# A transformer block on one core: norm groups of 2, 4, 4, 2, 1 and a new issue order

## The chip, the cores and the metric

One core of a Trainium2 chip. The kernel is written in Tile (Python that emits the instructions of each engine). The metric is the device time of one execution in microseconds; the median of the runs shown counts. Engines: PE (matmuls) with its weight loads (PEld), DVE (VectorE), ACT (ScalarE), POOL (GpSimd), SP (SyncE, which here only issues DMAs).

## The reference

Sequence 2048, width 512, 32 heads of 16, MLP width 1792 over the sequence axis, bfloat16.

```python
mod = (silu(c) @ w_mod).reshape(1, 6, 1, 512)            # sa, ca, ga, sb, cb, gb
h = layernorm(x) * (1 + ca) + sa
q, k, v = split_heads(h @ wqkv)
# each position attends to 8 positions of its past, 2 apart (0, 2, ..., 14 back), masked at the start
x = x + ga * (softmax(q . k[pos - off] * 16**-0.5) @ v[pos - off]) @ wo
h = layernorm(layernorm(x) * (1 + cb) + sb)
u = gelu(einsum('bsd,sf->bdf', h, w1) + b1)              # mixes along the sequence
x = x + gb * (einsum('bdf,fs->bds', u, w2) + b2).transpose
```

## The kernel before

The 16 tiles of 128 positions are worked in five chunks of 2, 4, 4, 4 and 2 tiles (`SIZES`). A chunk goes through the stages whose names are used below; the digits are chunk and part, or tile:

- ln1s, ln1v (statistics), rstd1, nb1, n1 (the first layer norm), then the transposition of the normed tiles: tr and hT by PE in chunks 0 and 1, xt by a transposing DMA on SP in chunks 2 to 4;
- qkv (12 groups of matmuls a chunk, in chunk 0 two parts each) and ev (its eviction from PSUM, on ACT or DVE); halo copies the last 16 positions of k and v to the next chunk;
- qk: the product of q with 8 shifted copies of k, one wide TENSOR_TENSOR on DVE per quarter of the width; red adds it up over the head on PE in psL; max, sub, exp, esum, rcp, smB form the softmax; a2 (a DMA on SP or ACT) spreads the weights over partitions, vd (a DMA on SP) lays out v;
- pv: the product of the weights with v on DVE, pvacc its sum on PE, oev its eviction, wo the output projection on PE, with one matmul more by the identity that adds the residual, x1 its eviction with the row sum (a DVE variant adds the residual itself, and then wo leaves that matmul out: flag n);
- ln2q (sum of squares), ln2m (variance), rstd2, nb2, n2, aff (scale and shift by the modulation), ln3s, ln3v, rstd3, nb3, h3: the two further layer norms. ln2m, rstd, nb and aff work on a group of `GRP[ch]` tiles at once; tiles 14 and 15 (`LN2D`) take their statistics with bn_stats instead of ln2q and ln2m.

The MLP's first product is summed over the sequence in sweeps (mlp1_sweep_column_tile), as h3 tiles become ready; park stores a partial sum, padd adds it again, gelu follows. mlp2 forms the 16 output tiles, fin adds bias, gate and residual, st_out stores.

The modulation: modcols on PE give shift and scale of the first norm as columns (a1col scales the weights: wsc; sab goes through qvb to the biases of q and v), modrow0 and modrow1 give the other rows, which go through DRAM (st_row, ld_row) to all partitions. modrow1 reads three of the six blocks of w_mod, loaded to a region of gT that the MLP later uses.

The order of all this is written out by hand in `ORDER`, one token per operation. Each engine issues its own operations in that order and waits in order; SP does so with its DMAs. A suffix a, d, p or s takes the variant on ACT, DVE, POOL or SP; q splits a matmul into four of 32 columns; n leaves out a matmul; fill:n is n matmuls of 128 columns without use. PSUM has six buffers of one bank (ps), SBUF four for the wide products (big) and five for vd, and a pool's buffer is taken in the order of ORDER. `schedule` (lines 86 to 125) turns ORDER into the program; lines 397 to 410 are rstd and nb, 459 to 461 the loads of w_mod's rows, 497 to 507 the halo, 560 to 594 the rows, 851 to 889 x1 to aff. Nearly every instruction is recorded under line 142, the wrapper that issues it, so the profile is read by tile names and by order.

## Time and profile before

| | us |
|---|---|
| median of 3 runs | 206.71 |
| lowest, highest | 206.41, 206.78 |
| profiled execution, its own time | 207.27 |
| its span in the profile | 205.6 |
| PE, DVE, ACT, POOL busy | 192.8, 160.4, 127.4, 21.1 |
| mean granted TensorE clock | 0.992 |

The span runs from the first to the last recorded instruction; the 1.7 us between it and the execution's time lie around it. Times in the views count from the start of the span. A busy PE is not a PE at its peak: a matmul of 512 columns is recorded with 379 ns, but one starts every 216 ns. An instruction's wait is shown in square brackets with the one that released it.

### The profile page before, as it was taken

Reading aid. Unit: us, or ns where it says so; the run is one execution under the profiler, and the core shown is the slowest. Engines: PE = TensorE matmul, PEld = TensorE weight load, DVE = VectorE, ACT = ScalarE, POOL = GpSimd, SP = SyncE. Lnnn points to the kernel's source line nnn. Section 1 sums busy time; section 2 is a strip of 40 time slices with the busy share of each in tenths; the row PEclk is TensorE's granted clock in tenths of the full one; section 3 lists DMA queues with packets and bytes.
Section 4 is the critical chain, followed back from the end, with each engine's and each line's share of the span. In section 5 each row is a group of like instructions: output and inputs, shape, how many; then the busy total and the mean of one; then the engine's idle time right before and its main releaser. Section 6 shows DMA issues by size and latency. Waiting matters only on the chain.

```text
span 205.6 us, 4632 instructions
## 1 busy us (share of the span) xinstructions
PE 192.8 (94%) x1852; PEld 99.5 (48%) x1852; DVE 160.4 (78%) x251; ACT 127.4 (62%) x305; POOL 21.1 (10%) x46
## 2 busy tenths in 40 slices
...
PEclk9969999999999999999999999999999999999999
...
GB/s 153 334 377 351 67 226 143 231 223 224 187 113 263 342 207 247 212 45 153 53 154 300 20 76 279 190 130 356 282 336 223 26 26 26 77 25 29 146 96 51
DMA packets 54945, 35.95 MB, mean 175 GB/s; under 512 B 24460, under 2 KB 52236, under 8 KB 54924
## 3 DMA queue, kind: packets, MB, share of 16 engines
...
q10 hardware_dynamic: 1368, 0.23, 0.8%
q8 instruction: 14, 0.23, 0.5%
...
## 4 chain that ended last, share of the span: by engine, by line
PE 49%; ACT 19%; DVE 14%; DMA 7%; issue 6%; POOL 2%; SPq 1%; ACTq 0%; DVEq 0%; POOLq 0%
PE psS L142 48%; DVE big L142 8%; ACT junk L142 4%; ACT h L142 3%; DMA hT<-h 3%; DVE h L142 3%; ACT v_sb L142 2%; DMA xx<-in_A_x_dram 2%; ACT xx L142 2%; ACT o_sb L142 2%; POOL h L142 2%; DMA a2sb<-lsb 1%; ACT q_sb L142 1%; ACT gT L142 1%; ACT k_f L142 1%
## 5 line engine op out<-in xcount | busy, mean ns | idle before, releaser
L142 PEld LDWEIGHTS <-wst 128*128 128x128 bf16 (+1 forms) x446 | 35.3, 102 | 34.5 <-issue 3.0
L142 PE MATMUL psS<-h,wst 128*128 128x512 bf16 (+1 forms) x296 | 50.3, 379 | 0.0
L142 DVE TENSOR_TENSOR big<-a2sb,vD 128x4096 bf16<-128x4096 bf16 (+1 forms) x20 | 36.7, 1860 | 2.2 <-PE psL L142 1.9
L142 DVE TENSOR_TENSOR big<-q_sb,k_f 128x4096 bf16<-128x4096 bf16 (+1 forms) x20 | 36.6, 1864 | 0.0
L142 PE MATMUL psS<-hT,w_qkv 128*32 128x512 bf16 (+3 forms) x432 | 29.7, 346 | 0.9 <-DMA hT<-h 0.9
L142 DVE SCALAR_TENSOR_TENSOR h<-psS,bcol,rows_bc 128x512 f32<-128x512 f32 (+2 forms) x18 | 12.4, 691 | 21.6 <-PE psS L142 21.4
L142 PEld LDWEIGHTS <-w_qkv 128*32 128x32 bf16 (+1 forms) x474 | 19.6, 108 | 17.5 <-issue 5.7
L142 PE MATMUL psS<-gT,big 128*128 128x512 bf16 x112 | 24.8, 379 | 0.0
L142 PEld LDWEIGHTS <-big 128*128 128x128 bf16 x144 | 12.0, 97 | 15.0 <-DMA big<-in_w_mod_dram 0.9
L142 PE MATMUL psS<-woq,o_sb 128*32 128x512 bf16 (+1 forms) x136 | 16.7, 380 | 1.0 <-ACT o_sb L142 1.0
L142 ACT ACTIVATE gT<-psS,bcol 128x512 bf16<-128x512 f32 x14 | 8.9, 687 | 8.4 <-DVE psS L142 8.4
L142 ACT ACTIVATE junk<-xx 128x512 bf16<-128x512 bf16 x20 | 12.6, 629 | 2.3 <-DMA xx<-in_A_x_dram 1.6
L142 ACT ACTIVATE h<-xx,nb,rs 128x512 bf16<-128x512 bf16 x16 | 13.0, 815 | 1.5 <-DVE nb L142 1.4
L142 DVE TENSOR_TENSOR h<-h,xx 128x512 bf16<-128x512 f32 (+2 forms) x18 | 11.4, 633 | 3.2 <-DMA out_dram<-h 2.6
L142 DVE BATCH_NORM_STATS2 st<-xx 128x6 f32<-128x512 bf16 x15 | 9.8, 681 | 5.1 <-DMA xx<-in_A_x_dram 5.1
L142 DVE TENSOR_TENSOR psS<-psS,gT 128x512 f32<-128x512 f32 x14 | 9.5, 697 | 4.8 <-PE psS L142 4.8
L142 PE MATMUL psS<-hT,wst 128*128 128x256 bf16 (+1 forms) x64 | 12.8, 361 | 0.0
L142 PEld LDWEIGHTS <-group 128*32 128x32 bf16 x288 | 7.2, 96 | 11.6 <-issue 4.5
L142 DVE TENSOR_TENSOR h<-h,rows_bc 128x512 bf16<-128x512 bf16 (+2 forms) x20 | 11.5, 582 | 1.3 <-POOL h L142 0.4
L142 POOL TENSOR_SCALAR h<-xx,rs,nb 128x512 bf16<-128x512 bf16 x7 | 7.4, 1061 | 49.0 <-DVE nb L142 49.0
L142 ACT ACTIVATE v_sb<-psS,qvb 128x512 bf16<-128x512 f32 (+1 forms) x20 | 11.1, 595 | 1.4 <-PE psS L142 1.3
L142 PE MATMUL psS<-big,group 128*32 128x512 bf16 (+1 forms) x160 | 9.8, 339 | 2.0 <-DVE big L142 1.9
...
## 6 DMA issues: line engine op xcount, KB each, us to landing
...
```

Of the source, the lines that this page charges most:

```text
L142: r = fn(*a, **k)
```

## The change

ORDER is replaced as a whole, and with it which engine takes which operation: 62 operations change engine. GRP goes from (2, 2, 4, 1, 1) to (2, 4, 4, 2, 1). ln2q gets a variant on DVE. ln2m works with sums scaled by D, so that a single tile needs one instruction; rstd2 then scales by -1/D^2. The rows of w_mod for modrow1 are loaded by four DMAs of 128 rows of 3 KB (one per 128 inputs) instead of three of 512 rows of 1 KB. The halo copies get one more key of order. wo10 and wo11 leave out the residual matmul. The fillers are 41 + 18 at the start (35 + 14 before), 4 and 10 in between (3 and 15), 26 at the end (7). In ORDER below, the stretches at the start, around the affine step of chunk 1, around the last products, and the end are kept.

```diff
ORDER = """
-ident ld_x_1_4 act_table ln1s4:d ld_x1 ld_x0 ld_x_1_2 ln1s1:d ln1v1 ln1v4 ld_wmod1 ld_c cps ln1s0:d ln1s5:a ln1v5
-fill:35 ln1v0 fill:14 ln1s2:d silu_exp consts rstd1_0 nb1_0 n1_0:a ln1s3:d n1_1:p ln1v2 ln1v3 silu_dve rstd1_1 nb1_1
-n1_5:d n1_4:d modcols1 tr0_0 a1col ld_x_2_8 n1_3:d n1_2:a tr1_0 hT0_1:a ln1s9:d ld_wqkv1 tr1_2 hT0_0:a hT1_0:d hT0_2:a
-ld_x_2_6 ln1s6:d hT0_3:a qkv0_12 hT1_3:a wsc1_1:p ld_wqkv0 hT1_2:a ld_x_3_12 ln1s7:d hT1_1:a ln1s8:d ln1v8 ev0_12:a
-ld_wmod0 wsc1_2:p wsc1_3:p ln1v7 ln1v6 qkv0_10 ld_x_3_10 ln1s13:d ln1v13 qkv1_13 wsc0_3:a ln1v9 ev0_10:a qkv0_02
-qkv1_01 wsc0_0:p modcols0 rstd1_2 wsc0_1:p ln1s12:d ln1v12 wsc0_2:a nb1_2 sab:a qvb0 qvb_cp0:a ev1_01:a qkv0_00
-ln1s10:d ln1s11:d qkv1_11 ld_wqkv2 qvb1 wsc1_0:p ev0_00:a ln1v10 wsc2_2:a ev1_11:a qvb_cp1:a ev0_02:d ln1v11 halo0
-rstd1_3 qk0_2 qk0_0 qkv1_03 ev1_03:a qk0_1 ld_wmod2 qk0_3 qkv0_22 ev0_22:a nb1_3 modrow0 mrows0:a ld_wmod4 qkv0_20:q
-n1_6:a red0_0 n1_10:a red0_1 ld_wmod3 red0_2 red0_3 mask ev0_20:a qk1_1 ev1_13:a qkv1_00 ev1_00:a qkv1_02 qkv1_10
-n1_12:a max0 n1_7:p sub0 exp0 ld_wmod5 modrow1 ev1_02:a xt6 ld_wo2 esum0 qk1_3 ld_x_4_14 vd0_0 vd0_3 n1_9:p rcp0 smB0
-qkv1_12 mrows1 n1_8:p ev1_10:a qk1_0 qkv1_20 qkv1_23 xt8 vd0_2 a2_0_2:s qkv1_21:q qkv1_22:q ev1_12:a qk1_2 n1_11:a
-a2_0_1:a red1_0 qkv2_10:q qkv2_00:q red1_1 a2_0_3:s a2_0_0:s pv0_2 ln1s15:a ev1_22:a ev1_23:a st_row0 red1_2 red1_3
-ln1v15 wsc2_1:a ev1_20:a qkv2_12 ev2_10:a qkv2_02:q halo_v1:p qkv2_11 pv0_0 vd0_1 ev2_00:a ev1_21:a max1 pvacc0_2 sub1
-pv0_3 ld_wo3 pv0_1 ld_w1_0_896 ev2_12:a pvacc0_3 pvacc0_0 pvacc0_1 ln1s14:a qkv2_03:q qk2_0 st_row1 wsc2_0:a exp1
-ev2_02:a ev2_11:a ld_wo0 ln1v14 ld_row0 wsc2_3:p ld_wo1 esum1 woq_s rcp1 qkv2_01 rstd1_4 qkv2_22:q ev2_01:a xt10
...
-oev2_3:a x1_4:a ln2q4 max3 sub3:q exp3 pv2_2 ld_w2_4 pv2_0 qkv4_10 rstd3_0 halo_v4:p pvacc2_2 esum3 oev2_2:a pv2_1
-qkv4_20:q ln2m4 rcp3 qkv4_00:q n2_2:a vd3_1 vd3_2 ev4_20:a ev4_10:a aff2 smB3 nb3_0 qkv4_22:q h3_0:p ev4_00:a pvacc2_0
-oev2_0:a rstd2_4 nb2_4 pvacc2_1 oev2_1:a wo7 wo9 ln3s3:d ln3v3 vd3_0 n2_5:d fill:15 n2_4:d ev4_22:a ln3s2:a ln3v2
-a2_3_3:a aff4 rstd3_2 nb3_2 x1_9:a wo6 ln3s5:d h3_1:a ln3s4:d wo8 ln3v5 h3_3:p h3_2:a mlp1_0_0_0 mlp1_0_6_0 ln2q9
-vd3_3 x1_6:a ln3v4 mlp1_0_2_0 a2_3_2:s mlp1_0_1_0 a2_3_0:s a2_3_1:s pv3_3 x1_7:a rstd3_4 pvacc3_3 ln2q6 nb3_4 h3_4:a
...
-ld_w1_0_1408 ln3s7:d mlp1_0_7_0:q ln3v9 ln3v7 mlp1_0_8_0:q ld_w2_3 ln3v8 ln3s6:a ln3v6 wo13:qn red4_0 x1_12:a rstd3_6
-red4_1 red4_2 red4_3 max4 mlp1_0_10_0 ln2q10 ln2m11 nb3_6 h3_7:p x1_13:d sub4 exp4 esum4 mlp1_0_9_0 ln2m10 h3_9:a
-h3_8:d ln2q12 rcp4 smB4 mlp1_0_11_0 h3_6:p mlp1_0_11_4 mlp1_0_11_8 vd4_0 vd4_3 rstd2_11 nb2_11 n2_11:d mlp1_0_8_4
-ln2m12 rstd2_10 vd4_1 mlp1_0_7_4 mlp1_0_7_8 a2_4_3:a nb2_10 a2_4_1:a n2_10:d aff10 rstd2_12 mlp1_0_8_8 mlp1_0_10_4
-mlp1_0_9_4 ln2q13 park0_7:a park0_8:a aff11 mlp1_0_12_0 ln2m13 rstd2_13 a2_4_2:s a2_4_0:s pv4_2 nb2_13 pv4_1 nb2_12
-pv4_0 pv4_3 ln3s11:a mlp1_0_9_8 mlp1_0_10_8 ln3s10:d n2_13:a mlp1_0_12_4 ln3v11 n2_12:a ln3v10 park0_9:a park0_10:a
-ld_w1_0_1664 aff13 aff12 mlp1_0_12_8 pvacc4_0 pvacc4_1 oev4_0:a ld_w1_1_0 pvacc4_2 pvacc4_3 oev4_2:a park0_11:a
-mlp1_0_13_0 wo15 x1_15 ln2s15 wo14 rstd3_10 nb3_10 rstd3_11 ln2v15 ln3s12:a ln3v12 mlp1_0_13_4 mlp1_0_13_8 h3_10:p
-x1_14 inj1_6:n park0_12:a rstd2_15 park0_13:a ln3s13:d nb2_15 ln2s14 ln3v13 rstd3_12 nb3_12 n2_15:a inj1_5:qn inj1_0:n
-mlp1_1_0_6 mlp1_1_0_10 ln2v14 rstd2_14 ld_w1_1_640 inj1_1:n mlp1_1_5_6 aff15 ln3s15:a nb2_14 park1_0:+ n2_14:p aff14
...
-fin8_0 st_out8_0 fin11_0 st_out11_0 st_out14_0 fin13_0 st_out13_0 fin12_0 mlp2_15_0 fin15_0 st_out12_0 st_out15_0
-mlp2_15_2 mlp2_15_1 fin15_2 fill:7 fin15_1 st_out15_2 st_out15_1
...
+ident consts act_table ld_x_1_4 ln1s5:d ld_c ln1v5 ln1s4:d ln1v4 cps ld_x1 ln1s1:a fill:41 ld_x_1_2 ln1v1 silu_exp
+silu_dve ln1s2:a ld_x0 ln1s0:d ln1s3:d halo0 ln1v0 rstd1_0 fill:18 ln1v3 ld_wmod1 ln1v2 rstd1_1 nb1_0 n1_1:a n1_0:d
+nb1_1 n1_2:d n1_3:d ld_x_2_6 ld_wqkv1 ld_x_2_8 modcols1 n1_4:a a1col tr0_0 hT0_1:a hT0_3:a hT0_0:a ld_wqkv0 n1_5:d
+ln1s6:d tr1_0 ln1s7:d hT0_2:a wsc1_0:p hT1_0:a wsc1_2:p tr1_2 ld_wmod0 ln1s9:d wsc1_3:p ln1s8:d ln1v9 ln1v8 ln1v7
+ln1v6 qkv0_12 ld_x_3_10 hT1_1:a qkv0_10 ev0_12:d hT1_2:a rstd1_2 nb1_2 hT1_3:a qkv0_02 wsc0_0:p ld_wqkv2 ln1s10:d
+modcols0 ln1s11:d ln1v10 n1_7:a sab:a ld_x_4_14 n1_6:a qkv0_00 qvb0 n1_9:a qvb_cp0:d ln1v11 qkv1_10 ld_x_3_12 ev0_02:d
+ev0_00:a ld_wo1 ld_b1 ld_wrow2 ev1_10:a qkv1_00 qkv1_13 qk0_2 qvb1 n1_8:a qk0_3 qkv0_22:q qkv0_20:q ev0_10:a ld_wo2
+qk0_0 ld_wo0 red0_0 ld_wo3 ev1_00:a qkv1_03:q ln1s13:a ev1_13:a qk0_1 qk1_0 ld_wmod2 ld_wrow0 qvb_cp1:a ev0_22:a
+qkv1_02:q wsc0_2:p red0_1 red0_2 ln1v13 ev1_03:a ev0_20:a ld_wrow1 ev1_02:a red0_3 mask max0 wsc0_1:p qk1_3 wsc1_1:p
+ln1s12:a xt6 ld_wrow3 qkv1_11:q ev1_11:a qkv1_01 vd0_2 ev1_01:a qk1_1 vd0_1 qkv1_12 ev1_12:a sub0:q exp0 wsc2_3:a
+qkv1_22:q vd0_3 modrow0 esum0:q rcp0 smB0 ln1s15:a xt8 a2_0_2:s red1_0 ln1s14:a qkv1_21 qk1_2 a2_0_3:s qkv1_20 ln1v12
+a2_0_0:s mrows0:a a2_0_1:s rstd1_3 st_row0 modrow1 mrows1 vd0_0 red1_1 nb1_3 red1_2 red1_3 ln1v14 qkv2_13 n1_10:a
+ln1v15 rstd1_4 ld_row0 n1_13:a max1 nb1_4 wsc0_3:p pv0_3 qkv2_00:q qkv1_23 ev2_13:a ev1_20:a ev2_00:a sub1 exp1
+ev1_22:a qkv2_10 qkv2_03:q st_row1 ev2_10:a pv0_1 ev2_03:a ld_b2 wsc2_1:a pv0_2 n1_12:p pvacc0_2 pvacc0_3 esum1
+ev1_23:a pv0_0 qkv2_12 qk2_0 rcp1 pvacc0_0 n1_11:p ev1_21:a pvacc0_1 smB1 qkv2_01:q woq_s qk2_3 xt10 xt12 qkv2_11:q
+oev0_2:a qkv2_02:q oev0_0:a wo0 a2_1_3:s halo_v1:p vd1_1 ev2_01:a ev2_12:a a2_1_1:s ev2_11:a qk2_1 wo1:q wsc2_2:a
...
+biascols_cp:a rcp3 qkv4_10:q ev4_12:a n2_2:a pv2_0 pvacc2_0 oev2_2:a pvacc2_3 ln3v0 vd3_3 smB3 a2_3_3:s a2_3_1:a
+qkv4_22 pv2_1 a2_3_0:s qkv4_00:q n2_4:a oev2_3:a rstd3_0 fill:10 oev2_0:a pvacc2_1 ev4_22:a oev2_1:a wo9:q a2_3_2:s
+wo6:q ev4_00:a aff2 ln3s4:a wo8:q pv3_1 pvacc3_1 ln3s5:d nb3_0 ln3s2:d ln3v4 ln3s3:a x1_8:a ln3v3 ln3v5 wo7 ln3v2
+rstd3_2 ev4_10:d x1_6:a nb3_2 h3_3:d h3_2:d pv3_2 h3_1:p h3_0:p h3_4:a mlp1_0_0_0 mlp1_0_2_0 vd3_0 vd4_3 ln2q6:a
+ld_w2_3 pv3_0 x1_9:a qk4_0 mlp1_0_6_0 oev3_1:a mlp1_0_1_0 ln2q8:a h3_5:a x1_7:a mlp1_0_0_4 ln2q7:a ln2q9:a vd4_0
+park0_0:a ln2m6 rstd2_6 mlp1_0_1_4 park0_1:a mlp1_0_2_4 mlp1_0_3_0 mlp1_0_3_4 park0_2:a ld_w1_0_896 red4_0 pvacc3_2
...
+ln3v8 ln3v7 ln3v6 vd4_2 mlp1_0_9_0:q ln3v9 ln2q12:a x1_10:d rstd3_6 nb3_6 h3_6:a ln2q10:a x1_13:d ln2q13:a esum4 rcp4
+x1_11:d h3_9:a ln2m12 rstd2_12 smB4 a2_4_0:a mlp1_0_8_0 ld_w1_0_1408 mlp1_0_10_0 ln2q11:d ln2m10 nb2_12 n2_13:d
+a2_4_3:a n2_12:d mlp1_0_7_0 h3_7:p mlp1_0_9_4 mlp1_0_7_4 mlp1_0_12_0 mlp1_0_8_4 a2_4_2:s aff12 rstd2_10 h3_8:p
+mlp1_0_8_8 mlp1_0_7_8 nb2_10 n2_10:a park0_7:a mlp1_0_12_4 a2_4_1:s pv4_3 mlp1_0_10_4 mlp1_0_10_8 n2_11:a pv4_0
+mlp1_0_9_8 mlp1_0_11_0 mlp1_0_11_4 pv4_2 pv4_1 aff10 ln3s11:d mlp1_0_11_8 park0_8:a park0_9:a park0_10:a park0_11:a
+pvacc4_0 pvacc4_2 pvacc4_3 oev4_2:a mlp1_0_12_8:q ln3s10:d ln3v10 ln3v11 pvacc4_1 oev4_0:a inj1_1:n ld_w1_0_1664
+mlp1_0_13_0 wo14 x1_14 ln3s12:a rstd3_10 mlp1_0_13_4 nb3_10 h3_10:p ln3v12 wo15 ld_w1_1_0 ln3s13:a ln2s14 ln2v14
+ld_w1_1_640 x1_15 rstd2_14 nb2_14 n2_14:p ld_w2_1 mlp1_0_13_8 inj1_3:n ln2s15 park0_12:a ln2v15 park0_13:a inj1_6:n
...
+fin8_0 st_out8_0 fin10_0 st_out10_0 mlp2_13_0 fin12_0 st_out12_0 st_out9_0 fin13_0 st_out7_0 mlp2_11_0 fin11_0
+st_out13_0 mlp2_14_0 fin14_0 mlp2_15_0 st_out11_0 mlp2_15_2 fin15_0 st_out14_0 fin15_2 st_out15_0 mlp2_15_1 fill:26
+st_out15_2 fin15_1 st_out15_1
...
"""
@@ -276,7 +276,7 @@
     ESD=(4,),
     RAW=(0, 1),
     LN2D=(14, 15),
-    GRP=(2, 2, 4, 1, 1),
+    GRP=(2,4,4,2,1),
     XDMA=(2, 3, 4),
     XG=2,
     INJ=(1,),
@@ -394,13 +394,13 @@
                                                op0=ALU.mult, op1=ALU.subtract, reverse1=True)
         add("dve", 0.15, fv, reads=[("stt", l, st)], writes=[("mv", l, st)], name=name[:3] + "v" + name[4:])
 
-    def ln_rstd(l, g0, n, name, var=None, vreads=None):
+    def ln_rstd(l, g0, n, name, vreads=None, vscale=1.0):
         mv, lv, rs, nb = (ln_t[k, l] for k in ("mv", "lv", "rs", "nb"))
         sl = slice(g0, g0 + n)
-        var = mv[:, sl, 1] if var is None else var
+        var = mv[:, sl, 1]
 
         def fa():
-            nc.scalar.activation(lv[:, sl, 0], var, ACT.Ln, bias=epscol[:, 0:1])
+            nc.scalar.activation(lv[:, sl, 0], var, ACT.Ln, scale=vscale, bias=epscol[:, 0:1])
             nc.scalar.activation(rs[:, sl, 0], lv[:, sl, 0], ACT.Exp, scale=-0.5)
         reads = [("mv", l, st) for st in range(g0, g0 + n)] if vreads is None else vreads
         add("act", 0.54, fa, reads=reads + ["ident", "act_table"], writes=[("rs", l, g0)], name="rstd" + name)
@@ -456,9 +456,8 @@
     dma(rowB, wmod_view[:, :, 2 * D:3 * D], D * D * 2, [], [("wst", 1)], "ld_wmod2")
     for l in range(4):
         dma(woq[32 * l:32 * l + 32, :, :], wo_view[l], 32 * 4 * D * 2, [], [("woq", l)], f"ld_wo{l}", rate=110e3)
-    for r in range(3):
-        dma(rowA[:, :, r * D:(r + 1) * D], wmod_view[:, :, (r + 3) * D:(r + 4) * D], D * D * 2, [], [("rowA", r)],
-            f"ld_wmod{r + 3}")
+    for kt in range(KT):
+        dma(rowA[:, kt, :], wmod_view[:, kt, 3 * D:6 * D], P * 3 * D * 2, [], [("rowA", kt)], f"ld_wrow{kt}", row=3 * D * 2)
     dma(b1_t[:], B_b1.rearrange("(t p) -> t p", p=P), 4096, [], ["b1_t"], "ld_b1")
     dma(b2_t[:], B_b2.rearrange("(t p) -> t p", p=P), 4096, [], ["b2_t"], "ld_b2")
 
@@ -502,8 +501,9 @@
         G.add_any([("pool", 0.4, lambda: nc.gpsimd.tensor_copy(v_, u_)),
                    ("act", 0.28, lambda: nc.scalar.activation(v_, u_, ACT.Identity)),
                    ("dve", 0.15, lambda: nc.vector.tensor_copy(v_, u_))],
-                  reads=[(nm, ch - 1, j) for j in range(4)],
-                  writes=[("kh", 3), ("kq", 2)] + [("k", -1, j) for j in range(4)] if nm == "k" else [("vh", ch), ("vh", ch - 2)],
+                  reads=[(nm, ch - 1, j) for j in range(4)] + [("vt", ch - 1)],
+                  writes=[("kh", 3), ("kq", 2)] + [("k", -1, j) for j in range(4)] if nm == "k" else
+                  [("vh", ch), ("vh", ch - 2), ("vt", ch - 2)],
                   name=f"halo_{nm}{ch}")
     add("pool", 2.0, mk_consts, writes=["consts", "mask"], name="consts")
     add("act", 1.3, lambda: nc.scalar.add_instruction(
@@ -571,7 +571,7 @@
                                              lhsT=sc[:, kt:kt + 1].to_broadcast([P, 32]),
                                              rhs=w_[:, kt, dt_ * P:(dt_ + 1) * P], start=(kt == 0), stop=(kt == KT - 1),
                                              tile_position=(0, 32 * dt_))
-            add("pe", 0.3 * nr, f_mm, reads=["sc", "gT_use"] + ([("wst", 1)] if r0 == 0 else [("rowA", i) for i in range(3)]),
+            add("pe", 0.3 * nr, f_mm, reads=["sc", "gT_use"] + ([("wst", 1)] if r0 == 0 else [("rowA", i) for i in range(KT)]),
                 alloc=s_, name=f"modrow{b_}", tiled=True)
 
             def src_(s_=s_, nr=nr):
@@ -858,8 +858,13 @@
                       name=f"x1_{st}").link = wo_
 
             def f(st=st):
-                nc.scalar.activation(junk[:], xx[:, st, :], ACT.Square, scale=D ** -0.5, accum_out=sums[:, st, 1:2])
-            add("act", 0.73, f, reads=[("xx", st)], writes=[("sum1", st)], name=f"ln2q{st}")
+                nc.scalar.activation(junk[:], xx[:, st, :], ACT.Square, scale=D ** 0.5, accum_out=sums[:, st, 1:2])
+
+            def fd(st=st):
+                nc.vector.scalar_tensor_tensor(junk[:], xx[:, st, :], float(D), xx[:, st, :], op0=ALU.mult, op1=ALU.mult,
+                                               accum_out=sums[:, st, 1:2])
+            G.add_any([("act", 0.73, f), ("dve", 0.83, fd)], reads=[("xx", st)], writes=[("sum1", st)], name=f"ln2q{st}",
+                      locks=True)
         for g0 in range(t0, t0 + nt, GRP[ch]):
             gn = min(GRP[ch], t0 + nt - g0)
             gt = range(g0, g0 + gn)
@@ -870,12 +875,15 @@
 
                 def f(g0=g0, gn=gn, mv=mv):
                     gs = slice(g0, g0 + gn)
-                    nc.vector.scalar_tensor_tensor(mv[:, gs, 0], sums[:, gs, 0], -1.0 / D ** 2, sums[:, gs, 0],
-                                                   op0=ALU.mult, op1=ALU.mult)
-                    nc.vector.tensor_tensor(mv[:, gs, 1], mv[:, gs, 0], sums[:, gs, 1], op=ALU.add)
-                add("dve", 0.4, f, reads=[("sum0", st) for st in gt] + [("sum1", st) for st in gt],
+                    if gn == 1:
+                        nc.vector.scalar_tensor_tensor(mv[:, g0, 1:2], sums[:, g0, 0:1], sums[:, g0, 0:1], sums[:, g0, 1:2],
+                                                       op0=ALU.mult, op1=ALU.subtract)
+                        return
+                    nc.vector.tensor_tensor(mv[:, gs, 0], sums[:, gs, 0], sums[:, gs, 0], op=ALU.mult)
+                    nc.vector.tensor_tensor(mv[:, gs, 1], mv[:, gs, 0], sums[:, gs, 1], op=ALU.subtract)
+                add("dve", 0.2 if gn == 1 else 0.4, f, reads=[("sum0", st) for st in gt] + [("sum1", st) for st in gt],
                     writes=[("mv", 1, st) for st in gt], name=f"ln2m{g0}")
-                ln_rstd(1, g0, gn, f"2_{g0}", vreads=[("mv", 1, st) for st in gt])
+                ln_rstd(1, g0, gn, f"2_{g0}", [("mv", 1, st) for st in gt], -1.0 / D ** 2)
             for st in gt:
                 ln_norm(1, g0, gn, st, h2[:, st - t0, :], xx[:, st, :], [("xx", st)], [("h2", ch % NH2, st - t0)], f"n2_{st}",
                         g0 not in LN2D)
```

47 lines of the change are left out of this document (23 added, 24 removed).

## The prediction

> **What bounds the kernel now.** I read four views: the busy table of the page, the chain that ended last, the busy time in chosen windows, and the timeline of single engines. Each engine takes its operations in the order in which ORDER lists them, so the trace's instructions can be matched to the names in ORDER one by one, engine by engine; names such as qk0_2 below come from that.
>
> The windows (busy us per engine, then granted clock, DMA share, GB/s):
>
> ```profile
> 9.00:20.00 11.00, 10.37 (x114) 8.14 (x114) 8.51 (x26) 8.16 (x19) 6.51 (x11) 0.84 1.09 365
> 20.00:36.00 16.00, 15.11 (x234) 8.82 (x236) 15.78 (x13) 14.81 (x33) 4.11 (x3) 1.00 0.75 152
> 36.00:60.00 24.00, 23.19 (x327) 11.00 (x322) 22.14 (x20) 18.72 (x42) 0.50 (x1) 1.00 0.79 189
> 60.00:88.00 28.00, 25.16 (x385) 13.27 (x377) 27.36 (x24) 26.96 (x67) 0.95 (x2) 1.00 0.83 251
> 88.00:124.70 36.70, 35.88 (x357) 16.18 (x358) 35.43 (x68) 34.18 (x93) 3.07 (x4) 1.00 0.48 117
> 124.70:202.00 77.30, 77.30 (x397) 36.58 (x397) 46.37 (x89) 20.18 (x47) 3.06 (x4) 1.00 0.53 148
> ```
>
> The columns are PE, PEld, DVE, ACT, POOL. See two stages. From 20 to 124.7 us DVE is busy 100.7 of 104.7 us; ACT is close behind from 60 on. From 124.7 PE is busy without a gap up to 202. The chain says the same of the end:
>
> ```profile
> 122.31 0.07 DVE nb L142
> 122.38 2.28 DVE big L142 x2
> 124.66 0.04 issue
> 124.70 77.24 PE psS L142 x392
> ```
>
> So the time is: start until DVE's first large product (qk0_2, 19.97), plus DVE's work and waits up to its last one (pv4_3, 123.43), plus the PE work still queued behind it, plus a tail of 3.8 us after the last matmul. PE in the first stage has gaps (adding the distances between matmul starts that exceed 0.216 us per 512 columns gives about 14 us from 11.5 to 125), but most of them wait for DVE or ACT.
>
> **The change, part by part.**
>
> *Code.* (a) Groups of four in chunk 1 and of two in chunk 3 remove three ln2m, three nb2, three nb3 on DVE, six Ln/Exp pairs on ACT (286 to 292 ns + 203 ns each), and put two affine steps into one. (b) The one-operation variance needs a group of one outside LN2D. Groups are now 2, 4, 4, 2, and chunk 4's tiles 14 and 15 are in LN2D, so it is never built: cost 0. The D factors only change constants. (c) The 3 KB rows move the same 1.5 MB in four DMAs instead of three; modrow1, their reader, ran at 28.07 when the last landed at 23.8, so it stays hidden, below a cost or gain of those 4.3 us. In the new order row 3 is issued behind the transpose xt6; if that cover went, modrow1 would stall PE at about 30 us, ahead of red1. (d) The extra "vt" key orders the halo copies only and emits nothing.
>
> *Start.* Before, the k, q groups and two chunk-1 groups precede qvb0 on PE (qkv0_12, qkv0_10, qkv1_13, qkv0_02, qkv1_01, modcols0), then qkv0_00 and ev0_02, and qk0_2 follows 1.7 us after qvb0's start (18.27). After, qkv1_13 and qkv1_01 are behind qvb0 (2 x 0.86 less) and qkv0_00 ahead of it (0.88 more): -0.85. Against that, x0 is now loaded after the 256 KB of x_1_2, at the place whose landing was 7.01 instead of 4.91; nb1_0 follows ln1s0, ln1s3 (2 x 0.60 start to start), aggregates and rstd1_0 (0.50), so n1_0 ends near 9.7, the transposes and four hT0 copies on ACT follow, and qkv0_12 starts near 12.1 rather than 11.53: +0.5. modcols0 had 0.4 us of inner gap; its weights are one 256 KB load nearer the head of the SP queue, so I take 0.3 off. Sum **-0.7** with the half clock as it was; bounds +0.5 (the late x0 alone) and -2.3 (next paragraph).
>
> The clock: the third slice of the page shows it.
>
> ```profile
> PEclk9969999999999999999999999999999999999999
> ```
>
> The record has it at half from 11.35 to 14.77 us, which cost 0.84 on qkv0_12 and 0.76 on qkv0_10, 1.6 us. It fell after a stretch in which PE had a gap of 1.7 us between filler and modcols1 and short ones in the transposes. After, 59 fillers instead of 49 reach to about 8.3 us, modcols1 can start when wmod1 lands (8.4; its other input, silu_dve, moved ahead of the norms), but then tr0_0 waits until 10.2. Busy time in 7.9 to 11.35 is about the same, so I keep the half clock as likeliest. [...]
>
> *DVE between qk0_2 and the last pv4.* Costs are start to start, as instructions overlap by some 0.08 us (product of 4096: 2.29 long, 2.20 apart). Gone from the stretch: aff4 1.22, aff10 and aff11 1.36, ln3s3, ln3s4, ln3s7 1.80, seven norms of 0.325 (2.28), seven tiny ones 0.74: 7.4. New: aff2 over four tiles +1.07 (a 2048-wide TENSOR_TENSOR is 1223 ns, a 1024-wide 690), aff12 for two tiles 1.22, ln3s2, ln3s6, ln3s8 1.80, five norms 1.63, x1_10, x1_11 and ln2q11 2.13 (scalar_tensor_tensor 684 ns plus accumulator read 84), ev4_10 0.61, two aggregates 0.18: 8.6. Net **+1.2**. The grouping saves DVE about 1 us; the order spends it on work taken from ACT. Bounds: 0.5 and 1.8.
>
> *DVE's waits there.* The largest:
>
> ```profile
> 31.41 4.48 DVE L142 TENSOR_TENSOR big<-q_sb,k_f 128x4096 bf16<-128x4096 bf16 x2
> 37.76 1.23 DVE L142 TENSOR_TENSOR big<-a2sb,vD 128x2048 bf16<-128x2048 bf16 x1 [1.88 <-PE psL L142]
> ```
>
> The page names psL; the SP row shows the true cause, the a2_0 stores issued behind a transpose and a vD copy:
>
> ```profile
> 29.05 1.52 SPq L142 DMA_TRANSPOSE hT<-h  x1
> 30.62 1.04 SPq L142 DMA_DIRECT2D vD<-v_sb  x1
> 31.76 2.89 SPq L142 DMA_DIRECT2D a2sb<-lsb  x3
> ```
>
> They landed at up to 37.2, 7 us after smB0 (30.70). After, n1_8 and n1_9 precede ev0_10 on ACT, so xt8 no longer waits for POOL and can go at about 27.4; x_4_14 and wo loads lie in the early HBM stretch; vd0_0 goes behind a2_0. I expect 3 to 4.5 us from smB0 to the landing, and DVE has qk1_2, mrows1 and max1 (2.2 + 0.8 + 1.1) ahead of its first pv0. So the 1.88 goes; next late is red1_3 for max1, about level. Other waits (0.36 at aff0, 0.31 at pv4_2, 0.19 at esum4) may come back elsewhere; pv3_1 right behind aff2 has only 4.5 us from smB3, against 4.6 needed before. I take **-1.4**, bounds +1.5 and -2.5.
>
> POOL now has n1_12 and n1_11 inside DVE's full stretch. Before, one such norm there was stretched:
>
> ```profile
> 27.62 2.80 POOL L142 TENSOR_SCALAR h<-xx,rs,nb 128x512 bf16<-128x512 bf16 x1
> ```
>
> against 0.77 elsewhere. Two of these are 5.6 us ahead of xt10 and xt12, so they land near 48; qkv3_00, their first reader, comes behind wo1, near 50, and red2_0 stands behind it on PE. Hidden, with 2 us to spare; DVE has three products to make before it lacks a buffer. [...]
>
> *PE behind the last pv4.* By the rows, matmuls from pvacc4's last group to the last of mlp2 sum to 76.8 before and 76.6 after (wo10 and wo11 leave out the residual matmul, 0.43, but ahead of this point): **-0.2**. The last 26 fillers are 1.5 us of PE against 3.8 us of store and end after it: 0. The order of mlp2 and of the w2 loads changes; mlp2_2, third, needs a load issued near 145 and landing before 153 and runs near 159.
>
> **Sum.** -0.7 + 1.2 - 1.4 - 0.2 = -1.1. The profiled execution took 207.27 (span 205.6 and 1.7 around it): 206.2. It lies 0.56 above the median of 206.71, so the forecast is 205.6.
>
> **Rivals.**
> 1. *Full clock.* The longer filler keeps the clock up through 11.35 to 14.77. For it: ten more fillers, modcols1 0.7 earlier. Against: x0 late, tr0_0 idle until 10.2. A further -1.4 (1.6 less what inputs would then hold back): 204.2.
> 2. *DVE becomes fuller (slower).* The a2_0 stores stay behind xt8 (both still share SP, and one store left the ACT queue for SP), so 1.88 stays, and the late x0 eats the start. The +1.2 then stands alone with -0.2: 207.7. It decides as soon as start and waits together bring less than 1.0. For it: DVE is 96% busy, so each moved operation counts in full.
> 3. *Parts cancel.* Start -0.7, waits -0.3: 206.7.
>
> **Chances.** Forecast 0.40 (204.9 to 206.4), rival 1 0.22, rival 2 0.23, rival 3 0.15. About 0.2% is what a measurement of this kernel can tell from no change. Faster 0.62, same 0.15, slower 0.23. The range takes in rivals 1 and 2 with a margin for the unknown waits: 203.9 to 207.9.
>
> **What would show it.** In the changed profile: qk0_2 at 19.3 (17.9 at full clock); DVE's first pv0 without a wait; last pv4 near 122.5; PE without a gap from there to the end, 76 to 77 us. The sum fails if PE shows new gaps behind the last pv4, if xt10 or xt12 hold PE at qkv3_00 long enough to starve DVE, or if modrow1 waits for row 3.

## The result and the profile after

| | before | after |
|---|---|---|
| median, us | 206.73 (206.41 to 206.78, 4 runs) | 203.87 (202.78 to 204.14, 4 runs) |
| ratio | | 0.9855 [0.9817, 0.9893] |
| span of the profiled execution | 205.6 | 202.4 |
| DVE's first large product, qk0_2, starts | 19.97 | 17.22 |
| last product pv4 starts | 123.43 | 119.63 |
| last matmul but the fillers starts | 201.71 | 197.74 |
| from there to the end of the span | 3.84 | 4.67 |

The gain, 2.86 us, is more than twice the forecast of 1.1. The rows of the table say where: 2.75 us up to qk0_2, 1.05 from there to the last pv4, 0.17 behind it; 0.83 is given back at the end. Together that is 3.14, as much as the spans, 205.55 and 202.41, differ. Executions more than 1.5% above the fastest of their kernel (14 of the kernel before and one of the changed kernel, all at a lowered clock) are left out of the counts and means below, not out of the medians.

The slices of the page of the changed kernel: where before had a 6 in the third, there is none.

```profile
PEclk9999999999999999999999999999999999999999
```

PE's own timeline of the changed kernel around the first groups (start, us, what, how many) gives the start:

```profile
11.47 2.93 PE L142 MATMUL psS<-hT,wst 128*128 128x256 bf16 x24 [0.20 <-ACT hT L142]
14.24 0.54 PE L142 MATMUL psS<-sc,big 128*128 128x1 bf16 x16
14.64 1.05 PE L142 MATMUL psS<-hT,wst 128*128 128x256 bf16 x8
15.52 0.67 PE L142 MATMUL psS<-sab,wst 128*128 128x1 bf16 x16
```

The first row is the groups from qkv0_12, the second modcols0, the last qvb0. From qkv0_12 to qvb0 it is 4.05 us; before it was 6.74 (11.53 to 18.27):

```profile
11.53 6.10 PE L142 MATMUL psS<-hT,wst 128*128 128x256 bf16 x32
...
18.27 0.67 PE L142 MATMUL psS<-sab,wst 128*128 128x1 bf16 x16 [0.26 <-ACT sab L142]
```

DVE's timeline of the changed kernel in the stretch where before lost 1.88 us ahead of its first pv0:

```profile
27.90 2.29 DVE L142 TENSOR_TENSOR big<-q_sb,k_f 128x4096 bf16<-128x4096 bf16 x1 [0.91 <-ACT q_sb L142]
...
35.40 4.65 DVE L142 TENSOR_TENSOR big<-a2sb,vD 128x2048 bf16<-128x2048 bf16 x4
```

The four pv0 run in one piece with no bracket; a wait of 0.91 is new, in front of qk1_1. SP's rows show the a2_0 stores:

```profile
27.71 2.47 SPq L142 DMA_TRANSPOSE hT<-h  x1
30.56 2.67 SPq L142 DMA_DIRECT2D a2sb<-lsb  x4
```

The transpose xt8 still stands ahead of them, but it is through when smB0 ends at 30.53, and the stores follow at once. Before, SP's first a2_0 store went out 1.06 us after the end of smB0.

The windows of the changed kernel, in the columns of the prediction:

```profile
9.00:20.00 11.00, 10.39 (x144) 8.58 (x148) 9.78 (x25) 10.64 (x22) 5.40 (x8) 1.00 1.07 322
...
60.00:88.00 28.00, 25.84 (x444) 13.66 (x440) 27.69 (x22) 26.56 (x67) 2.93 (x2) 1.00 0.73 217
...
107.00:124.70 17.70, 17.70 (x134) 8.26 (x130) 17.02 (x42) 13.98 (x36) 1.59 (x3) 1.00 0.53 126
124.70:198.00 73.30, 73.30 (x372) 34.81 (x370) 42.52 (x76) 17.46 (x37) 3.02 (x4) 1.00 0.51 144
```

PE is full already from 107 on, not only from 124.7. The chain of waits says the same:

```profile
107.12 0.21 PE psL L142 x4
107.33 92.08 PE psS L142 x518
```

Before, the last unbroken piece was 77.24 us of 392 matmuls.

### The profile page after: what moved, and what is told of

The parts are those of the page before. It is cut to its first block, busy times and chain, and to the rows that moved or that the text cites. A ratio compares the mean times of both kernels' runs of the same rounds, so it can differ in the third digit from the quotient of the medians.

```text
span 202.4 us, 4973 instructions
## 1 busy us (share of the span) xinstructions
PE 191.6 (95%) x2031; PEld 100.4 (50%) x2031; DVE 159.3 (79%) x237; ACT 127.9 (63%) x299; POOL 20.5 (10%) x45
## 4 chain that ended last, share of the span: by engine, by line
PE 52%; DVE 21%; ACT 11%; DMA 6%; SPq 5%; issue 4%; POOL 0%; DVEq 0%; ACTq 0%
PE psS L142 51%; DVE big L142 16%; SPq L142 5%; DMA xx<-in_A_x_dram 5%; ACT v_sb L142 2%; ACT q_sb L142 2%; ACT junk L142 2%; ACT k_f L142 1%; DVE m L142 1%; DMA a2sb<-lsb 1%; ACT lsb L142 1%; ACT o_sb L142 1%; DVE mv L142 1%; DVE woq L142 1%; DVE st L142 1%
## 5 line engine op out<-in xcount | busy, mean ns | idle before, releaser
L142 ACT ACTIVATE junk<-xx 128x512 bf16<-128x512 bf16 x25 | 15.7, 629 | 3.5 <-DMA xx<-in_A_x_dram 2.9
L142 ACT ACTIVATE h<-xx,nb,rs 128x512 bf16<-128x512 bf16 x19 | 15.0, 807 | 1.6 <-DVE nb L142 1.1
L142 PEld LDWEIGHTS <-ident 128*32 128x32 bf16 (+1 forms) x236 | 11.0, 107 | 3.8 <-issue 2.3
L142 PE MATMUL psS<-hT,wst 128*32 128x512 bf16 (+2 forms) x100 | 11.5, 346 | 0.2 <-ACT hT L142 0.2
L142 DVE BATCH_NORM_STATS2 st<-xx 128x6 f32<-128x512 bf16 x12 | 7.8, 682 | 4.5 <-DMA xx<-in_A_x_dram 4.5
L142 ACT ACTIVATE q_sb<-psS,qvb 128x512 bf16<-128x512 f32 (+1 forms) x18 | 10.9, 622 | 0.7 <-PE psS L142 0.7
L142 DVE TENSOR_TENSOR h<-h,rows_bc 128x1024 bf16<-128x1024 bf16 (+2 forms) x14 | 10.7, 766 | 0.3
```

Source lines behind the costliest of these rows:

```text
L142: r = fn(*a, **k)
```

## The experiments

**How they are compared.** Several chips were used, and the kernel before differs between them by up to 0.8 us, so a kernel is compared on its own chip. The records of each execution show one more thing. Its mean granted clock is either 0.996 and more, or 0.992 and less. The five kept profiles of the second kind each show one window of 3.41 us at half speed. I call the two kinds full and half and give their means apart, with the number of them.

| chip | before, full | before, half | after, full | after, half |
|---|---|---|---|---|
| 14 | 205.24 (16) | 206.13 (16) | | |
| 10 | 205.21 (8) | 206.80 (12) | 203.74 (10) | 204.13 (1) |
| 6 | 204.78 (13) | 206.05 (10) | | |
| 9 | 205.60 (7) | 206.71 (9) | 203.14 (4) | none |
| 7 | 205.28 (5) | 206.80 (3) | 203.50 (4) | 205.25 (2) |

The kernel before is half in 50 of 99 executions, the changed one in 3 of 25 (the 22 others include the four of the result, 203.66). In the kernel before, half executions take 0.9 to 1.6 us longer. At full clock on both sides the change is worth 1.5, 2.5 and 1.8 us on the three chips.

**The two kernels again** (c_before, c_after, c_after_b, c_after_c; no edit).

> The kernel before, unchanged, to see whether its half clock is a habit or an accident. Theory (the start, half of it by the clock): the granted clock falls to half for one stretch of 3.4 us between about 11 and 15 us again, qk0_2 starts near 20.0, and the time stays within 0.2% of 206.7. Rival (accident): the clock stays full here, qk0_2 starts near 18.4, and the time is the same 206.7 or up to 1.6 less; then the clock can't explain a difference between medians.

c_before: 206.09 median, ratio 1.0017 [0.9979, 1.0055], 5 full (205.59), 5 half (206.54): the half clock is neither a habit nor an accident, it comes in every second execution. The profiled one was full, with qk0_2 at 18.52 and last pv4 at 122.27; the stretch between them stays (103.75; 103.46 in the profile before). PE's rows show what the half window cost:

```profile
11.20 4.76 PE L142 MATMUL psS<-hT,wst 128*128 128x256 bf16 x32
...
16.60 0.67 PE L142 MATMUL psS<-sab,wst 128*128 128x1 bf16 x16 [0.26 <-ACT sab L142]
```

From qkv0_12 to qvb0 it is 5.40 us at full clock, against 6.74: the half window is worth 1.34 us there. f_before59 below, also full, has 5.41.

> The changed kernel, unchanged, to have it on the same chip as the others and in many executions. In the first four kernels the executions of one kernel fell into two sets by granted clock: about 206.3 where it was at half once (mean clock 0.992 and below), about 205.3 where it was not. Theory (clock plus order): the changed kernel is never or hardly ever at half, and at full clock it is still 1 to 1.5 us under the kernel before at full clock, so 203.8 to 204.3. Rival (the clock is all): at full clock it equals the kernel before at full clock, 205.0 to 205.4.

c_after: 204.02, ratio 0.9877 [0.9847, 0.9907]. At full clock it takes 203.74, far below the 205.0 to 205.4 of the rival that the clock is all.

> The changed kernel unchanged, as the measure for the two runs beside it: 203.7 to 204.2 by both theories, at full clock in nearly all executions.

> The changed kernel unchanged, beside t_after7_b: 203.1 to 204.0 by both theories; Theory A: 0.4 to 0.9 above t_after7_b, Theory B: within 0.3 us of it.

c_after_b: 203.14, ratio 0.9858 [0.9804, 0.9913]. c_after_c: 204.05, ratio 0.9887 [0.9828, 0.9947]. Adding up the time not covered by any DVE instruction between qk0_2 and the last pv4 gives 4.0 and 4.3 us in the two profiles of before, 2.6 in the first profile after, and 1.3, 1.5 and 2.2 in c_after, c_after_b and c_after_c. So the new wait of 0.91 ahead of qk1_1 belongs to that one execution; in c_after_b it is 0.19. In c_after_c a wait ahead of the first pv0 is back, 0.86 us for the landing of an a2_0 store.

**The clock: ten fillers** (f_before59 on before's ORDER, f_after49 the reverse on the new one).

```diff
-fill:35 ... fill:14
+fill:41 ... fill:18
```

> The kernel before with 41 + 18 fillers in place of 35 + 14, nothing else. Theory that the ten fillers keep the clock up: no half clock at 11 to 15 us, qk0_2 near 18.4, 205.1 to 205.6. Rival that the norms and transposes decide, or where the clock's window lies: half clock as before, qk0_2 near 20.0, 206.5 to 206.9.

> The changed kernel with the old fillers, 35 + 14 in place of 41 + 18. Theory (ten fillers keep the clock up): half clock in about half of the executions, those about 1 us longer, the median 0.3 to 1.0 above the changed kernel. Rival (the earlier modcols1 keeps it up): no half clock, same time as the changed kernel.

f_before59: 205.16, ratio 0.9988 [0.9956, 1.0020]; 11 of 12 full (205.14). f_after49: 204.98, ratio 0.9959 [0.9920, 0.9997]; 8 of 11 half (205.32), 3 full (204.0). Both came out as their theory had it. With either order the ten fillers change how often the clock halves: with 59 in 1 of 12 and 3 of 25, with 49 in 8 of 11 and 50 of 99. Over all other runs below it is 8 of 84 with 59, and 7 of 12 with 49 (s_beforestart). Nothing else shows in the time: f_before59 at full is before at full (205.24).

The windows at the clock's own edges show where it happens. The profile before:

```profile
7.94:11.35 3.41, 1.98 (x39) 1.77 (x40) 3.13 (x13) 3.05 (x7) 1.43 (x3) 1.00 1.05 361
11.35:14.77 3.42, 3.42 (x21) 2.50 (x19) 3.35 (x11) 3.38 (x7) 3.24 (x5) 0.50 1.11 381
```

f_before59:

```profile
7.45:10.86 3.41, 2.93 (x54) 2.55 (x53) 3.12 (x13) 3.05 (x8) 0.91 (x2) 1.00 1.04 355
10.86:14.27 3.41, 3.41 (x28) 2.75 (x26) 3.26 (x11) 3.41 (x7) 3.28 (x6) 1.00 1.09 373
```

The changed kernel:

```profile
7.37:10.78 3.41, 2.76 (x50) 2.20 (x47) 2.92 (x12) 2.82 (x8) 0.11 (x1) 1.00 1.01 334
10.78:14.19 3.41, 3.21 (x33) 2.96 (x31) 3.00 (x10) 3.38 (x9) 3.34 (x6) 1.00 1.10 387
```

Two more profiles with 59 fillers, c_after:

```profile
6.45:9.87 3.42, 2.08 (x40) 1.68 (x37) 2.73 (x11) 2.47 (x10) 0.00 (x0) 1.00 1.02 342
9.87:13.28 3.41, 3.27 (x27) 3.02 (x28) 3.41 (x10) 3.10 (x8) 1.99 (x3) 0.50 1.08 378
```

and g_split1, of which more below:

```profile
6.22:9.63 3.41, 2.02 (x42) 1.74 (x39) 2.55 (x10) 2.26 (x9) 0.00 (x0) 1.00 0.94 302
9.63:13.04 3.41, 3.08 (x36) 2.63 (x36) 3.14 (x8) 3.41 (x9) 1.71 (x3) 1.00 1.08 378
```

The second column is PE's busy time, the number after POOL the clock. In the five profiles that have a half window, PE was busy in the window ahead of it for 1.44 (s_beforestart), 1.57 (t_after7), 1.98, 2.08 and 2.38 us (f_after49). But 2.02 us in g_split1 were not followed by a half window, nor 2.13 in c_before, nor, later in the execution, 1.67 in g_split3 (from 117.65) and 1.69 in f_after49 (from 61.96). So the recorded busy time does not decide. Counting instead the columns that a window's matmuls stream, against 512 in 216 ns (a quarter of that, counted so by me, for matmuls that the rows show as 128*32 instead of 128*128), gives 24 to 38% ahead of the five half windows and 37% or more ahead of all others; this is my estimate from the records and orders them nearly, not fully. That the fillers make the half window rare is shown by the counts; what the clock goes by is not. Where the windows lie differs from execution to execution (edges at 7.94, 7.45, 7.37, 6.45 and 6.22 here), and the same kernel is now full, now half.

**The start alone and the rest alone** (s_afterstart: new ORDER up to qk0_2, with ld_wmod4 in the place of ld_wrow2, then before's remaining tokens in before's order; s_beforestart: the mirror, with 35 + 14 fillers).

```diff
 # s_afterstart, on before
-ident ld_x_1_4 act_table ... qk0_2  (before's start, 35 + 14 fillers)
+ident consts act_table ... qk0_2    (the new start, 41 + 18 fillers)
```

> The new order up to and with qk0_2 (its fillers, loads, norms, engines), then the old order and the old groups for all that is left. Theory (the start): qk0_2 starts near 17.2 and most of the 2.75 us reach the end: 204.0 to 204.5. Rival (the rest: groups, other engines, fewer waits between qk0_2 and the last pv4): the old rest absorbs the early start, 206.0 to 206.7.

> The mirror: the old order up to and with qk0_2, then the new order with the new groups. Theory (the start): 206.0 to 206.7, with qk0_2 near 20.0 if the clock falls as before, near 18.4 and 205.0 if not. Rival (the rest): 204.0 to 204.5 although qk0_2 is late.

> The kernel before with the new order up to qk0_2 alone, again, for a profile of it (the profile of the first such run was of an execution of 1103 us and says nothing). Median near 205.2. Theory A (the start's gain is given back in the old middle, where something not tied to the start ends last): qk0_2 near 17.2 as in the changed kernel, last pv4 at 121.0 to 122.3, so a stretch between them of 104 to 105 us against 103.5 before. Theory B (the gain is kept to the last product and lost behind it): last pv4 near 120.7, stretch 103.5, and more PE time or a longer tail behind it.

(The profiled execution of s_afterstart took 1103 us, was disturbed, and is not used; s_afterstart_b is the same kernel again.) s_afterstart: 205.22, ratio 0.9965 [0.9936, 0.9994], 11 executions, all full (205.12). s_afterstart_b: 205.16, ratio 1.0003 [0.9972, 1.0035], 10, all full (205.29). s_beforestart: 205.23, ratio 0.9987 [0.9954, 1.0019], 5 full (204.99), 7 half. At full clock neither half of ORDER gains more than 0.3 us, and on the chip of s_afterstart_b the new start alone is 0.5 slower than before (204.78); the whole gains 1.5 to 2.5. So s_afterstart lies between its theory and its rival. DVE's timeline of s_afterstart_b shows what happens to the earlier start:

```profile
17.82 1.23 DVE L142 TENSOR_TENSOR big<-q_sb,k_f 128x2048 bf16<-128x2048 bf16 x1
19.02 0.69 DVE L142 BATCH_NORM_STATS2 st<-xx 128x6 f32<-128x512 bf16 x1
...
24.88 2.29 DVE L142 TENSOR_TENSOR big<-q_sb,k_f 128x4096 bf16<-128x4096 bf16 x1 [0.70 <-PE psL L142]
27.09 0.68 DVE L142 TENSOR_REDUCE m<-psL 128x64 bf16<-128x512 f32 x1
```

qk0_2 is 0.7 us ahead of c_before's (and 0.1 ahead of f_before59's, 17.89); max0, at 27.09, is behind its 25.34. In before's order two statistics of chunk 3 (1.6 us with their aggregates) precede qk0_2 on DVE; the new start leaves them behind it, and the new middle gives them to ACT, which the old middle doesn't. Then DVE waits 0.70. The last pv4 comes at 122.31 as in c_before (122.27), after a stretch of 104.49: theory A. In s_beforestart, whose profiled execution was half, DVE's timeline has the counterpart, waits in the new middle behind the old start: 1.60 for ACT's eviction of q, and 1.11 ahead of the first pv0:

```profile
26.06 2.29 DVE L142 TENSOR_TENSOR big<-q_sb,k_f 128x4096 bf16<-128x4096 bf16 x1 [1.60 <-ACT q_sb L142]
...
39.55 3.49 DVE L142 TENSOR_TENSOR big<-a2sb,vD 128x2048 bf16<-128x2048 bf16 x3 [1.11 <-issue]
```

**x0 first** (x_x0first).

```diff
-... fill:41 ld_x_1_2 ln1v1 silu_exp silu_dve ln1s2:a ld_x0 ln1s0:d ...
+... fill:41 ld_x0 ld_x_1_2 ln1v1 silu_exp silu_dve ln1s2:a ln1s0:d ...
```

> The changed kernel with the load of x0 put ahead of that of the 256 KB of x_1_2, where the old order had it. The prediction charged the late x0 with 0.5 us up to the first product. Theory A (that charge is real but was covered by other gains): qk0_2 0.3 to 0.6 us earlier, the time 0.3 to 0.6 us below the changed kernel beside it. Theory B (x0's statistics wait only 0.25 us for it, and nb1_0 then waits for ACT): within 0.25 us of the changed kernel.

203.92, ratio 0.9897 [0.9842, 0.9951]; 3 full at 204.0, against 203.14 (4) of c_after_b beside it. Both theories failed: the early x0 came out 0.9 us slower, by three executions against four. Its qk0_2, 17.77, is 0.3 behind c_after_b's, less than the start varies between the full profiles of the changed kernel (17.22 to 18.51), so the profiles don't show all of the 0.9. DVE's timeline of x_x0first:

```profile
7.02 0.69 DVE L142 BATCH_NORM_STATS2 st<-xx 128x6 f32<-128x512 bf16 x1 [0.24 <-DMA xx<-in_A_x_dram]
...
8.60 0.22 DVE L142 SCALAR_TENSOR_TENSOR mv<-mv,st 128x1 f32<-128x1 f32 x1 [0.67 <-ACT junk L142]
9.02 0.16 DVE L142 SCALAR_TENSOR_TENSOR nb<-mv,rs 128x2 f32<-128x2 f32 x1 [0.20 <-ACT rs L142]
```

x_1_2 now lands last, and its statistics are on ACT, which DVE waits for: nb1_0 at 9.02 instead of 8.46 (8.58 in c_after_b). The order of the two loads fits the engine that reads each.

**Rows of 1 KB** (r_1kb).

```diff
-    for kt in range(KT):
-        dma(rowA[:, kt, :], wmod_view[:, kt, 3 * D:6 * D], P * 3 * D * 2, ...)
+    for r in range(3):
+        dma(rowA[:, :, r * D:(r + 1) * D], wmod_view[:, :, (r + 3) * D:(r + 4) * D], D * D * 2, ...)
```

> The changed kernel with the rows of w_mod loaded again by three DMAs of 512 rows of 1 KB in place of four of 128 rows of 3 KB, at the places of the first three. The prediction's step: no effect, their reader modrow1 runs some us after the last has landed; within 0.3 us of the changed kernel, 203.7 to 204.4. Rival: the loads share the DMA engines with x, wqkv and wo in the first 30 us, and the 1 KB rows take longer, so that qk0_2 or the first products move: 204.8 or more with qk0_2 unchanged and modrow1 or max1 later.

203.28, ratio 0.9881 [0.9845, 0.9918], 9 full (203.32). That lies inside what the changed kernel itself shows from chip to chip (203.14 to 203.74); the rows are worth nothing that can be told.

**The groups** (g_split: second and fourth chunk taken apart; g_split1, g_split3: one of them). Each token of ln2m, rstd2, nb2, aff, rstd3, nb3 of the group is followed at once by that of the split-off part:

```diff
-    GRP=(2,4,4,2,1),
+    GRP=(2,2,4,1,1),    # g_split;  (2,2,4,2,1) g_split1;  (2,4,4,1,1) g_split3
-... ln2m12 rstd2_12 smB4 ...
+... ln2m12 ln2m13 rstd2_12 rstd2_13 smB4 ...
```

> The changed kernel with the old groups of 2, 2, 4, 1, 1, the split operations next to each other in the new order; ln2m of the single tiles is now one operation. Theory (DVE sets the time to the last product): by the rows, start to start, chunk 1 costs DVE 0.45 more and chunk 3 about 0.3 more ahead of the last product, ACT six pairs of Ln and Exp more: 0.5 to 1.0 us longer than the changed kernel. Rival (the waits hide it): within 0.3 us of it.

> The changed kernel with only the second chunk's group of four taken apart into pairs again (twins placed right behind each other). With both chunks' groups taken apart the kernel took 208.6 us against 204.0 with the groups, 4.7 more, while the removed instructions themselves are worth only about 0.5 to 1.0 us of DVE. Theory A (the loss is the fourth chunk's, where the MLP's products wait for tiles 10 to 13 right behind the last pv4): within 0.4 us of the changed kernel, 203.8 to 204.5; last pv4 near 119.6 and PE without a gap behind it. Theory B (the loss comes from the DVE stage as a whole, in proportion to the added instructions): 205.5 to 206.5, with last pv4 later than 120.5.

> The changed kernel with only the fourth chunk's pairs taken apart into single tiles (which brings the variance in one operation to life for tiles 10 to 13). Theory A: nearly the whole loss, 208.0 to 208.8; last pv4 near 121 and gaps of 1 to 2 us each on PE between 115 and 140. Theory B: 206 to 207. If it takes under 205, the loss needs both chunks together.

g_split: 208.68, ratio 1.0126 [1.0083, 1.0169], 5 full at 208.57, 4.8 above the changed kernel on that chip; expected were 0.5 to 1.0. g_split1: 205.01, ratio 0.9975 [0.9930, 1.0021], 9 full at 204.79, between its two theories. g_split3: 207.31, ratio 1.0109 [1.0042, 1.0176], all four full, 207.55; also between its two. Beside r_1kb on the same chip (203.32) g_split3 is 4.2 worse and g_split1 1.5. So most of it sits in the fourth chunk; the two add up to more than the 4.8 of both together. DVE's timeline of g_split3 ahead of the last products:

```profile
117.33 4.63 DVE L142 TENSOR_TENSOR big<-a2sb,vD 128x2048 bf16<-128x2048 bf16 x4 [1.78 <-issue]
```

DVE is 1.2 us ahead of the changed kernel at max4 (104.96 against 106.17) and 1.1 us behind it here. What it waits for are the weights a2_4, two of whose stores ACT issues, behind one of its two extra Ln and Exp pairs (0.42 us). g_split3's ACT queue:

```profile
112.59 1.36 ACTq L142 DMA_DIRECT2D a2sb<-lsb  x2
```

and its SP queue, which issues a load of w1 at 113.11:

```profile
111.67 1.34 SPq L142 DMA_DIRECT2D a2sb<-lsb  x2
113.11 4.96 SPq L142 DMA_DIRECT2D wst<-in_B_w_dram  x3
```

ACT's second store, a2_4_3, goes out at 113.26, 0.15 behind that load, and lands 3.63 us later. In the changed kernel it goes out at 114.07, 0.25 ahead of the load, and lands after 2.06. Whether its place behind the load is what its landing goes by, these two numbers alone don't show. To test it, g_split3_sp moves this one store to SP, ahead of the load, and keeps the rest:

```diff
-a2_4_3:a
+a2_4_3:s
```

> The changed kernel with the fourth chunk's pairs taken apart into single tiles, as in g_split3, and with one store of the fifth chunk's weights (a2_4_3) issued from SP instead of ACT. In g_split3 ACT's two more Ln and Exp pairs put that store at 113.26 us, 0.15 behind SP's issue of a 512 KB load (in the changed kernel it is 0.25 ahead of it); it landed 3.63 us later instead of 2.06, and DVE waited 1.78 us for its last products. Theory A (this tie is what the split costs up to the last product): the wait goes, pv4_3 begins 1.2 to 1.8 us earlier after smB4 than in g_split3, and the time is 205.5 to 206.5. Theory B (the loss is the number of small instructions on DVE and ACT, wherever they wait): the wait moves, pv4_3 stays where it was against smB4, and the time is 207.0 to 207.8.

205.71, ratio 1.0002 [0.9957, 1.0046], 9 full at 205.80, 2.7 above c_after_b on its chip, where g_split3 was 4.2 above r_1kb: theory A. DVE's timeline of g_split3_sp:

```profile
115.11 4.63 DVE L142 TENSOR_TENSOR big<-a2sb,vD 128x2048 bf16<-128x2048 bf16 x4
```

No bracket; from smB4 to the first pv4 it is 4.34 us (110.77 to 115.11) instead of 6.11, and the store landed after 1.98. (The edit also takes the issue of the store off ACT's queue; that is not told apart from its place ahead of the load.) Of the 2.7 us that are left, the profiles of g_split3_sp and c_after_b show 0.4 between qk0_2 and the last pv4 and 1.5 behind it (79.61 us to the last matmul against 78.13). PE has gaps there where the changed kernel has none:

```profile
131.86 10.30 PE L142 MATMUL psS<-h,wst 128*128 128x512 bf16 x46 [1.09 <-DVE gT L142]
```

By the profile it waits for an addition into gT on DVE, a park. DVE reaches it at 131.13, and in the changed kernel at 130.60, although the last pv4 began 1.1 us later there. In 124.7 to 141 PE is busy 15.00 of 16.3 us in g_split3_sp, 16.30 in the changed kernel. The remaining 0.8 us were not traced. In g_split1 the profile showed the four a2_0 stores taking 3.82 us to issue on SP instead of 2.67 and a wait of 1.55 in front of the first pv0. That is far ahead of the group it splits, the executions reach from 203.3 to 206.25, and c_after_c, where nothing is split, waits 0.86 us there; so whether the split causes it stays open.

**The end** (t_after7, t_after7_b; b_best with the 1 KB rows as well).

```diff
-... mlp2_15_1 fill:26 st_out15_2 ...
+... mlp2_15_1 fill:7 st_out15_2 ...
```

> The changed kernel with 7 fillers behind the last matmul instead of 26. In the profile of the changed kernel the issue of the last store but one took 1.26 us instead of 0.33, and the tail after the last matmul was 4.6 us instead of 3.8. Theory (an accident of that execution): no difference in the median, within 0.3 us. Rival (the 26 fillers, or their loads of instructions, hold SP up): 0.5 to 0.8 us shorter.

> The changed kernel with 7 fillers at the end instead of 26, and with the rows of w_mod in three loads of 1 KB rows. The 7 fillers gave 0.76 us at full clock, the 1 KB rows nothing that can be told from 0 across chips (203.3 on one chip beside 203.7 of the changed kernel on another). Theory A (only the fillers count): 0.6 to 0.9 below the changed kernel beside it. Theory B (the 1 KB rows bring 0.4 more): 1.0 to 1.3 below. No row of the profile of the changed kernel shows a wait on these loads, so A.

> The changed kernel with 7 fillers at the end instead of 26, again, with the changed kernel beside it in more rounds. On one chip it took 202.98 at full clock beside 203.74; on another, together with the 1 KB rows, 203.18 beside 203.14. Theory A (the 26 fillers cost the end what their late SP issue shows, 0.3 to 1.2 us of tail): 0.4 to 0.9 below the changed kernel beside it. Theory B (the slow issue comes and goes and is not worth a median): within 0.3 us.

t_after7: 202.91, ratio 0.9851 [0.9802, 0.9901], full 202.98 (5) against 203.74 (10) of c_after. t_after7_b: 203.13, ratio 0.9839 [0.9779, 0.9899], full 202.81 (4) against 203.50 (4) of c_after_c. b_best: 203.75, ratio 0.9875 [0.9833, 0.9918], full 203.18 (7) against 203.14 (4) of c_after_b. The SP row of the last stores, changed kernel:

```profile
197.99 1.26 SPq L142 DMA_DIRECT2D out_dram<-h  x1
```

and t_after7_b:

```profile
197.71 0.33 SPq L142 DMA_DIRECT2D out_dram<-h  x1
```

Of twelve profiles with 26 fillers eleven have one of the last two issues at 0.64 to 1.52 us and a tail of 4.3 to 5.1 behind the last matmul (s_beforestart is the exception, 0.33 and 3.9); all with 7 have 0.33 and 3.8 to 4.0. So the slow issue goes with the fillers; the tail is 0.3 to 1.2 us longer, and two of three comparisons of the time give 0.7 us, the third nothing. As the full executions of one kernel here lie up to 2.4 us apart, a gain in time is not shown by these. Why PE's fillers slow an issue on SP was not found. The changed kernel with 7 fillers at the end has the lowest mean that was seen (202.81), with the same reservation.

## Why the prediction was wrong, point by point

| step | forecast | measured |
|---|---|---|
| start, up to qk0_2 | -0.7 | -2.75 |
| DVE's work to the last pv4 | +1.2 | +0.4 |
| DVE's waits there | -1.4 | -1.4 |
| PE behind the last pv4 | -0.2 | -0.17 |
| end | 0 | +0.8 |
| span | -1.1 | -3.14 |

**Start: the step that failed.** "Busy time in 7.9 to 11.35 is about the same, so I keep the half clock as likeliest" is wrong. In that stretch PE's busy time rose from 1.98 to 2.73 us, and the half window went, which took 1.34 us off the start (6.74 against 5.40 from qkv0_12 to qvb0). f_before59 and f_after49 show that the ten fillers alone make the half window rare. The reading had two faults: it took a window's place in one execution for a property of the kernel, and it weighed gaps in a fixed stretch by eye. The other error was the late x0, charged with +0.5: x0 landed at 6.41, not 7.01, n1_0 ended at 9.07 rather than 9.7, and qkv0_12 started at 11.47 rather than 12.1. What the order itself gives was about right: 5.40 - 4.05 is 1.35 us between qkv0_12 and qvb0, for the 0.85 and 0.3 forecast. A single profile says no more than that, for at full clock qk0_2 lies anywhere from 16.91 to 18.51 in the eleven profiles with the new start, and at 17.89 and 18.52 in the two with the old. And a start gained is only kept if the middle is made for it, as s_afterstart shows; the sum of independent terms had no place for that.

**The clock.** The result came out as in rival 1, 204.2, which had a chance of 0.22: 203.87 is 0.3 from it. The clock was as that rival had it; that the number is so close is partly luck, for start and DVE's work together came out about 1.5 better than in its sum, and the end gave 0.8 back. In the records the edges of the clock's windows lie 3.41 us apart (7.94, 11.35 and 14.77 in the profile before), and elsewhere in each execution (7.37 and 10.78 in that of the changed kernel). In the five profiles with a half window the clock fell after windows in which PE was busy 1.44 (s_beforestart), 1.57 (t_after7), 1.98, 2.08 (c_after) and 2.38 us (f_after49); by what it falls no run shows.

**DVE's work.** The time covered by DVE instructions rose from 99.46 to 99.85 us; +1.2 was over-counted by 0.8, just beyond its lower bound of 0.5. Start to start, x1_10, x1_11 and ln2q11 cost 1.80, not 2.13. And smB0, which took 0.77 beside POOL's stretched norm, takes 0.33 now; the sum did not have that. The rest are small differences both ways.

**DVE's waits.** Right, and for the reason given: the 1.88 ahead of the first pv0 is gone, as xt8 no longer holds up the a2_0 stores; qk1_1's 0.91 is what came next in that execution. That the size was met is partly chance: over the two profiles of before and the four after, the gain lies between 1.4 and 3.0, and in c_after_c 0.86 of the forecast wait is there. The two norms moved to POOL took 0.78 each and starved nothing.

**The groups.** Priced at about 1 us of DVE saved. With the new order they are worth 4.8: the order was made for them, and where the split operations stand, on ACT ahead of a2_4's stores and on DVE behind the last pv4, counts for more than what they take themselves. What the groups are worth in the old order was not run.

**Right:** the rows (0), the one-operation variance (not built), PE behind the last pv4, no gap on PE from there. **Mis-sized:** the 26 fillers, put at 0 because they end before the last store; they go with a slower issue of one of the last two stores, and the tail grew by 0.83.

The baseline may add to it: the four executions of before, 206.41 to 206.78, lie where its half executions lie (their clock is not on record), and the four after were full. Over many executions the difference is smaller or larger by chip: medians of 206.78 and 204.02, of 206.49 and 203.14.
